# Cosine attention followed by a gated two-layer block on one core: new order tables for all engines

## The chip, the core and the metric

The kernel runs on one core of one Trainium2 chip. A core has a matrix engine (PE, with its weight loads shown apart as PEld), a vector engine (DVE), a scalar engine that evaluates functions (ACT), a slower general engine (POOL), and a queue engine (SP) that here issues only transfers. Every engine works through its own instruction list in order, and lists meet only at semaphores. The metric is the device time of one execution in microseconds, the median of several runs.

## The reference

```python
q, k, v: (8, 12, 448, 64) float32, tau = 0.1
q_n = q / (norm(q) + 1e-6);  k_n = k / (norm(k) + 1e-6)
attn = softmax(q_n @ k_n^T / tau)            # per batch and head, 448 x 448
x = (attn @ v) laid out as (8*448, 12*64)    # 3584 tokens x 768
h = x @ w_in                                 # 768 -> 2048
out = (h * cos(h)) @ w_out                   # 2048 -> 768, float32
```

## The kernel before

**Units of work.** A quad is a group of four heads of one batch, so there are 24 quads (numbers 0 to 23), three to a batch. For each quad q and k are loaded (`load_one`, L447, SP's queue) and v too (`load_v`, L461, POOL's queue); they are squared (`square`, L487), summed (L509), turned into inverse norms by a few tiny instructions (`inverse`, L516: ACT L527 and L539, DVE L542 and L545), scaled (`scale`, L547) and turned by a transfer (`turn`, L595). Then come seven steps of `scores` (L608), each four matmuls on PE (L619) and one exponential on ACT (L627), and seven steps of `attend` (L639, PE L646), whose result ACT or DVE copies out of PSUM (L656 or L659). The row sums of quads 0 to 5 are formed by `spread` (L663, PE L672) and inverted on ACT (L685, L689); those of later quads by rounds of two quads (`sums`, L726, PE L735), after DVE has added some of the exponential tiles up (`add_up`, L704, L722). POOL or DVE multiplies the sums' inverse in (L762), which gives x.

**Chunks.** A chunk is one batch of 448 tokens, numbers 0 to 7. Its first matmul (M1, L784) makes 16 blocks of 128 features in pairs. Each pair goes through ACT L797, DVE L799, ACT L801 and DVE L803, which leave h*cos(h) in `gT`. Its second matmul (M2, L815) makes 6 or 8 output blocks of 128 tokens by 384, 16 matmuls each; each finished block is copied to `osb` by ACT (L824) or DVE (L827) and stored. M2 blocks use PSUM banks 6 and 7; scores, spread and attend steps take the other three pairs of banks in turn (`next_pair`, L882), so that a step needs the bank pair of the third step before it to have been read out.

**Weaving.** While M2 of chunk c runs, PE also does the scores and attends of quads that a later chunk needs. `stream` is the list of slots: s is one scores step, v all seven attend steps of the quad before, z its spread. For chunk c the table `VISITS[c]` has pairs (n, m): do the next n slots, then m matmuls of M2 (L1163 to L1171). `LATER` moves the v and z of a quad within the slots of the next quad (L878). A round of sums is put in where L1139 and L1168 allow it. PE's order after the start is thus written down by these tables. The order on the other engines after the start comes from a planner (`pass_`, L144), which walks the operations with assumed durations and picks for each engine the operation that can start first, with a priority that follows from when PE needs it. `ENG` says on which engine an operation lies: keys `s0:q` and `s1:q` are the squares of q and k of quad q (POOL without an entry), `n0`/`n1` their scaling (POOL, and DVE for n1 of quads 4 to 7), `a` the copy of the attend result (DVE), `x` the last multiplication (POOL, DVE for quad 8), `o:t:h` the copy of output block h of tile t (DVE). `TREE` says how many exponential tiles of a quad DVE adds up ahead of its round: 0 leaves seven tiles to sum on PE, 4 leaves three, 5 two, 6 one.

**The start.** Until M1 of chunk 0 (quads 0 to 2 are done there whole), every engine's order is written out by hand (L936 to L1087). Operations are numbered in the order in which they are written, `MOVE` adds a number to some of them (L91), and each engine's list is sorted by the result (L137, L157). All POOL transfers keep such a place too. Weights come in four transfers of w_in (`load_w1`, L469) and four of w_out (`load_w2`, L477) on POOL's queue. The loads of quad 5 wait for the second transfer of w_out (L1037), those of quad 6 for the third and fourth (L1091).

```python
        if key is None:
            self.count += 1
            key = self.count - 1
            if self.strict:
                key += MOVE.get(key, 0)
...
        for n, more in plan[1:]:
            visit(stream[:n])
            del stream[:n]
            if due and at[0] >= 2 * NNB and 1 <= at[0] % NNB <= 12:
                round_(due.pop(0), 13 - cur[0])
            fill(more)
```

## Time and profile before

| quantity | value |
|---|---|
| median of 3 runs | 417.64 us (416.97 to 417.76) |
| the profiled execution's own time | 417.37 us |
| its span, first to last instruction | 415.6 us |
| PE busy | 406.9 us |
| ACT busy | 313.7 us |
| DVE busy | 306.6 us |
| POOL busy | 199.6 us |
| granted PE clock | 1.00 |

A share of busy time is a mean over stages. The table of stretches gives it for a chosen stretch; the list by time gives single instructions, merged where the same line repeats; the number in brackets behind a row is the engine's idle time ahead of it, and what ended that. PE rows overlap a little, because matmuls are pipelined.

### The profile page before, as it was taken

How to read it: one execution, taken by the hardware profiler on the slowest of the kernel's cores; microseconds unless marked ns; L12 is line 12 of the kernel's file. 1: busy time of each engine (PE TensorE's matmuls, PEld its weight loads, DVE VectorE, ACT ScalarE, POOL GpSimd, SP SyncE). 2: the span in 40 equal slices, each digit the busy share in tenths (PEclk: the TensorE clock that was granted, in tenths of full speed). 3: DMA queues.
4: the chain of work that ended last, by engine and by line, in shares of the span. 5: the costliest groups of instructions: out<-in, count | busy, mean ns of one | idle time of the engine just before them, and what ended most of it. 6: DMA issues, size and time to landing. Idle time of an engine off the chain costs nothing.

```text
span 415.6 us, 8581 instructions
## 1 busy us (share of the span) xinstructions
PE 406.9 (98%) x3600; PEld 217.5 (52%) x3601; DVE 306.6 (74%) x368; ACT 313.7 (75%) x417; POOL 199.6 (48%) x132
## 2 busy tenths in 40 slices
PE   7999999999999999999999999999999999999996
PEld 6674544445554455454555555454555555555563
DVE  4958997879853669963899899964988479836931
ACT  5998889988888987878878667889886667715700
POOL 3866329793386862688715495088504050030000
PEclk9999999999999999999999999999999999999999
DMA  8999999986099999199939689299803350071033
GB/s 267 231 244 209 236 225 275 217 180 152 4 205 168 262 236 237 40 177 244 188 113 176 132 181 219 33 162 211 178 2 82 77 108 22 1 165 39 0 77 76
DMA packets 71399, 62.83 MB, mean 151 GB/s; under 512 B 40512, under 2 KB 66240, under 8 KB 71360
## 3 DMA queue, kind: packets, MB, share of 16 engines
q1 hardware_dynamic: 60688, 50.09, 52.3%
q0 software_dynamic: 10240, 11.80, 17.6%
q8 instruction: 28, 0.46, 0.5%
q10 hardware_dynamic: 432, 0.39, 0.3%
q14 instruction: 11, 0.09, 0.1%
HBM read 45.61 MB, written 11.01 MB: 136 GB/s over the span
## 4 chain that ended last, share of the span: by engine, by line
PE 88%; ACT 8%; DVE 1%; DMA 1%; issue 0%; SPq 0%; DVEq 0%
PE PS L815 35%; PE PS L784 35%; PE PS L619 8%; PE PS L646 6%; ACT E L627 5%; PE PS L735 2%; PE PS L672 1%; DMA Kf<-in_k_dram 1%; ACT E L634 1%; ACT ar L689 1%; ACT ar L685 1%; PE PS L582 0%; DVE n L509 0%; DVE AVs L659 0%; DVE Qn L553 0%
## 5 line engine op out<-in xcount | busy, mean ns | idle before, releaser
L815 PE MATMUL PS<-W,gT 128*128 128x384 bf16 (+2 forms) x895 | 156.4, 327 | 0.1
L627 ACT ACTIVATE E<-PS 128x896 f16<-128x896 f32 x161 | 137.0, 917 | 21.8 <-PE PS L619 21.2
L784 PE MATMUL PS<-xT,W 128*128 128x448 bf16 x768 | 147.0, 352 | 0.0
L815 PEld LDWEIGHTS PS<-W,gT 128*128 128x128 bf16 x896 | 83.2, 98 | 69.1 <-issue 15.2
L784 PEld LDWEIGHTS PS<-xT,W 128*128 128x128 bf16 x768 | 74.7, 98 | 70.0 <-issue 0.4
L797 ACT ACTIVATE ar<-PS 128x896 int32<-128x896 f32 x64 | 58.2, 911 | 32.1 <-PE PS L784 31.4
L799 DVE SCALAR_TENSOR_TENSOR ar<-ar,PS 128x896 f32<-128x896 int32 x64 | 69.0, 1084 | 17.9 <-ACT ar L797 17.7
L803 DVE TENSOR_TENSOR gT<-PS,ar 128x896 bf16<-128x896 f32 x64 | 69.3, 1088 | 4.9 <-ACT ar L801 4.3
L801 ACT ACTIVATE ar<-ar 128x896 f32<-128x896 f32 x64 | 60.5, 947 | 16.0 <-DVE ar L799 15.3
L762 POOL TENSOR_TENSOR xT<-AVs,R 128x896 bf16<-128x896 f32 x17 | 37.9, 2231 | 57.4 <-DMA R<-Zs 57.4
L827 DVE COPY osb<-PS 128x384 f32<-128x384 f32 (+2 forms) x56 | 31.1, 554 | 41.6 <-PE PS L815 40.7
L505 POOL TENSOR_TENSOR sqq<-Qf 128x896 bf16<-128x896 f32 x21 | 35.3, 1680 | 44.4 <-DVE n L509 35.1
L619 PE MATMUL PS<-qT,kT 64*64 64x448 bf16 x672 | 51.0, 360 | 2.1 <-ACT E L627 1.2
L553 POOL TENSOR_TENSOR Qn<-Qf,rr 128x896 bf16<-128x896 f32 x20 | 37.9, 1897 | 29.7 <-DVE rr L545 25.7
L722 DVE TENSOR_TENSOR E<-E 128x1792 f16<-128x1792 f16 (+2 forms) x26 | 36.5, 1403 | 4.7 <-PE PS L646 4.5
L646 PE MATMUL PS<-E,Vb 64*64 64x448 f16 x672 | 37.7, 350 | 0.0
L505 POOL TENSOR_TENSOR sqk<-Kf 128x896 bf16<-128x896 f32 x17 | 30.5, 1797 | 13.6 <-DVE n L509 10.7
L553 POOL TENSOR_TENSOR Kn<-Kf,rr 128x896 bf16<-128x896 f32 x17 | 31.2, 1835 | 6.0 <-DVE Qn L553 3.6
L659 DVE COPY AVs<-PS 128x896 f32<-128x896 f32 x21 | 22.8, 1087 | 11.7 <-PE PS L646 11.5
L619 PEld LDWEIGHTS PS<-qT,kT 64*64 64x64 bf16 x672 | 16.3, 105 | 28.0 <-issue 11.3
L509 DVE TENSOR_REDUCE n<-sqq 128x14 f32<-128x896 bf16 (+2 forms) x23 | 23.7, 1035 | 6.8 <-POOL sqq L505 6.0
L646 PEld LDWEIGHTS PS<-E,Vb 64*64 64x64 bf16 x672 | 20.0, 107 | 11.8 <-ACT E L627 0.9
(57 smaller groups left out, 232.8 us busy)
## 6 DMA issues: line engine op xcount, KB each, us to landing
out_dram<-osb SPq DMA_DIRECT2D x54, 192.0 KB, 3.0
Qf<-in_q_dram SPq DMA_DIRECT2D x23, 448.0 KB, 5.1
Kf<-in_k_dram SPq DMA_DIRECT2D x23, 448.0 KB, 5.1
R<-Zs SPq DMA_DIRECT2D x72, 112.0 KB, 3.0
Vb<-in_v_dram POOLq DMA_DIRECT2D x24, 224.0 KB, 5.2
W<-in_moe_w_in_dram POOLq DMA_DIRECT2D x4, 768.0 KB, 17.3
W<-in_moe_w_out_dram POOLq DMA_DIRECT2D x4, 768.0 KB, 25.1
qT<-Qn SPq DMA_TRANSPOSE x20, 4.3
```

What stands on the lines that cost most here:

```text
L505: op(eng, (1.68 if eng == "pool" else 1.05) * n, lambda e: e.tensor_tensor(dst, src, src, ALU.mult), r=cut(nm + "f", s, part), w=own, afte ...
L553: lambda e: e.tensor_tensor(n[0].ap()[:, j0:j1].rearrange("p j r d -> p r j d"), f[s].ap()[:, :, j0:j1], rb, ALU.mult),
L619: ins = e.matmul(bank(bs + r, S, 64 * a, 64 * a + 64), kT[u].ap()[64 * r:64 * r + 64, j, a, :], qT[u].ap()[64 * r:64 * r + 64, :, a, :], s ...
L627: act("exp", 0.81, lambda e: e.activation(E.ap()[:, es], two(bs), ACT.Exp, bias=SHIFT, scale=INV_TAU), r=pair(bs), w=[("E", es)], chain="E")
L646: ins = e.matmul(bank(bk + a, S, 64 * r, 64 * r + 64), Vb[vs].ap()[64 * a:64 * a + 64, r, j, :], E.ap()[64 * a:64 * a + 64, es, r, :], sta ...
L762: op(eng, 2.04 if eng == "pool" else 1.05, lambda e, u=u, sl=sl, b=b, c0=c0: e.tensor_tensor(xT[b % 2].ap()[:, c0:c0 + 2, :], AVs[sl].ap() ...
L784: ins = e.matmul(bank(bk + i2), W1.ap()[:, i, 128 * nb:128 * nb + 128], xT[c % 2].ap()[:, i, :], start=(i == 0), stop=(i == NKC - 1))
L797: op("act", 0.815, lambda e: e.activation(ar[s].ap().bitcast(I32), two(bk), ACT.Identity, bias=0.25, scale=INV2PI), r=bs, w=[("ar", s)], a ...
L799: op("dve", 1.005, lambda e: e.scalar_tensor_tensor(ar[s].ap(), ar[s].ap().bitcast(I32), -2.0 * math.pi, two(bk), ALU.mult, ALU.add), r=bs ...
L801: act("sin", 0.86, lambda e: e.activation(ar[s].ap(), ar[s].ap(), ACT.Sin, bias=GUARD * math.pi / 2.0, scale=GUARD), r=[("ar", s)], w=[("a ...
L803: op("dve", 1.01, lambda e: e.tensor_tensor(gT.ap()[:, 2 * pr:2 * pr + 2, col:col + S], two(bk), ar[s].ap(), ALU.mult), r=bs + [("ar", s)] ...
L815: ins = e.matmul(bank(bk, x1 - x0), gT.ap()[:, f, col:col + 128], W2.ap()[:, f, x0:x1], start=(f == 0), stop=(f == NNB - 1))
```

## The change

Five tables get new values; no instruction is written anew and no wait is written by hand.

- `VISITS` and `LATER`: other cuts of the same slots. Written out with s, v and z, chunk 1 for example ends before with ... [s s v10 s] 4 [s s] 6 [s s] and M1, and after with ... [s] 7 [s s] 9 [s s v10 s s s s s] 4 and M1. Chunk 0 begins with 23 instead of 25 matmuls of M2. Chunk 4 has [s v19 s s], a round, [s s] where it had [s s v19 s s], a round, [s s s] (the rounds are put in by L1168). A run of slots between two runs of M2 counts as one trip; there are 51 trips in both tables (11, 11, 6, 8, 7, 8 before; 10, 12, 6, 8, 7, 8 after, by chunk).
- `ENG`: 19 of the 56 output copies and 6 of the 21 attend copies go from DVE to ACT. Eight scalings, five last multiplications and four squares go from POOL to DVE. Of the four squares on ACT three go to POOL and one to DVE; one other goes from POOL to ACT.
- `TREE`: quad 22 gets 6 for 5, quad 12 gets 4 for 3.
- `MOVE`: every operation of the start gets a number. On SP, k of quads 3, 4 and 5 is loaded before q. On ACT, in the chain of inverse norms of quad 0, the last step for q (L536) goes ahead of the first for k, and the two last tiny steps for the second half of k (L534 and L536) go ahead of the first exponential, where they were behind the second and third. The two tiny steps of quad 3 (L527, L539) go ahead of the inversion of quad 2's sums (L685, L689), where they were behind it. On PE, the last spread of quad 2 goes behind its last attend. On POOL, the loads of v of quads 1 and 2 go behind two of the weights. The transfers of weights go out in the order w_in 2, 3, w_in 1, w_out 2, w_in 4, w_out 3, w_out 1, and w_out 4 only after three squares of quads 3 and 4; v of quad 3 goes out ahead of w_out 3 instead of behind all weights.

```diff
 VISITS = [
-    [(0, 25), (3, 12), (3, 11), (3, 3), (3, 5), (3, 12), (3, 10), (3, 4), (3, 4), (3, 0), (3, 4), (3, 5), (1, 1)],
-    [(0, 20), (3, 11), (3, 13), (3, 13), (3, 0), (3, 15), (3, 11), (3, 8), (6, 0), (3, 16), (2, 11), (4, 4), (2, 6),
-        (2, 0)],
-    [(0, 26), (2, 11), (3, 0), (2, 20), (4, 11), (3, 9), (2, 10), (5, 0), (3, 2)],
-    [(0, 21), (3, 9), (3, 11), (3, 8), (2, 8), (4, 26), (4, 17), (2, 12), (3, 11)],
-    [(0, 19), (3, 7), (3, 7), (2, 15), (3, 9), (3, 12), (2, 17), (5, 0), (2, 0), (1, 12)],
-    [(0, 25), (4, 15), (3, 21), (3, 15), (5, 24), (3, 7), (1, 10), (4, 8), (2, 14)],
+    [(0, 23), (3, 15), (3, 6), (2, 5), (5, 4), (2, 12), (3, 7), (2, 8), (5, 8), (6, 5), (3, 0)],
+    [(0, 23), (3, 5), (2, 16), (3, 8), (2, 4), (3, 0), (3, 14), (2, 10), (3, 11), (5, 12), (3, 6), (1, 7), (2, 9), (8,
+        4)],
+    [(0, 22), (3, 11), (2, 0), (3, 18), (3, 3), (2, 14), (3, 19), (5, 0), (3, 2)],
+    [(0, 19), (3, 10), (3, 12), (2, 0), (1, 8), (2, 7), (4, 28), (4, 20), (3, 12), (2, 7)],
+    [(0, 19), (3, 13), (3, 18), (3, 16), (4, 11), (3, 10), (2, 5), (4, 0), (2, 15)],
+    [(0, 25), (4, 6), (3, 14), (3, 17), (4, 26), (3, 23), (3, 9), (2, 10), (3, 10)],
     [],
     [],
 ]
...
-LATER = {18: -1, 5: 3, 7: -1, 21: -1, 9: 4, 10: -2, 12: 0, 23: 2, 15: -2, 13: -1, 22: 2, 8: 1, 16: 2, 14: 0, 17: -1,
-    19: -1, 20: 0}
+LATER = {18: -2, 5: 3, 7: -2, 21: 0, 9: 4, 10: -2, 12: -1, 23: 5, 15: -2, 13: 0, 22: 2, 8: 0, 16: 2, 14: 0, 17: -1,
+    19: 1, 20: 1, 3: -1, 4: 0, 11: 0}
...
-MOVE = {49: 2.0, 100: -6.5, 94: -4.0, 199: 5.5, 198: 3.0, 48: -155.0, 123: 23.0, 33: -18.5, 21: -15.0, 149: -9.5, 143:
...
+    18: 3.664, 19: 6.11, 20: 8.62, 21: 4.938, 22: 7.615, 23: 9.894, 24: 16.08, 25: 22.556, 26: 2.596, 27: 6.258, 28:
+    6.866, 29: 7.474, 30: 8.082, 31: 13.382, 32: 13.99, 33: -14.07, 34: 13.598, 35: 14.206, 36: 2.802, 37: 5.33, 38:
+    1.63, 39: -16.508, 40: 6.77, 41: 8.584, 42: 1.17, 43: 2.93, 44: -10.022, 45: 4.926, 46: 5.534, 47: 6.142, 48:
...
+    96: -9.342, 97: -6.424, 98: -2.99, 99: 3.888, 100: -14.752, 101: -5.45, 102: -15.69, 103: 2.63, 104: -26.57, 105:
+    -14.19, 106: 76.208, 107: -9.122, 108: -7.662, 109: -9.364, 110: -6.842, 111: -13.962, 112: -5.89, 113: -6.236,
...
-ENG = {'s1:13': 'act', 's1:21': 'act', 's1:22': 'act', 's1:23': 'act', 'o:3:1': 'dve', 'n1:12': 'dve', 'o:5:1': 'dve',
-    's0:15': 'pool', 's1:14': 'pool', 's0:20': 'pool', 'o:14:0': 'dve', 'o:16:1': 'dve', 'n0:20': 'pool', 'n1:19':
-    'pool'}
-TREE = {12: 3, 11: 0, 13: 0, 16: 4, 14: 6, 15: 6, 17: 4, 18: 2, 19: 0, 23: 6, 20: 6, 22: 5, 21: 6}
+ENG = {'s1:13': 'pool', 's1:21': 'dve', 's1:22': 'pool', 's1:23': 'pool', 'o:3:1': 'act', 'n1:12': 'dve', 'o:5:1':
+    'act', 's0:15': 'pool', 's1:14': 'dve', 's0:20': 'pool', 'o:14:0': 'dve', 'o:16:1': 'act', 'n0:20': 'pool',
+    'n1:19': 'pool', 'o:2:0': 'act', 'a:8': 'dve', 'n1:8': 'pool', 's0:9': 'pool', 'o:3:0': 'dve', 'o:6:0': 'act',
...
+    's1:10': 'pool', 'x:7': 'pool', 'n1:10': 'pool', 'a:7': 'dve', 's0:11': 'pool', 'n1:9': 'dve', 'n1:16': 'pool',
+    'x:12': 'pool'}
+TREE = {12: 4, 11: 0, 13: 0, 16: 4, 14: 6, 15: 6, 17: 4, 18: 2, 19: 0, 23: 6, 20: 6, 22: 6, 21: 6, 10: 0, 8: 0, 9: 0}
```

2 lines of the change are left out of this document (added), and 40 rows, old and new, of tables (ENG, MOVE).

## The prediction

> **What bounds the kernel now.** I read the page's busy times and the shares of the chain that ended last, then that chain in order of time, then the table of stretches. The page:
>
> ```profile
> PE 406.9 (98%) x3600; PEld 217.5 (52%) x3601; DVE 306.6 (74%) x368; ACT 313.7 (75%) x417; POOL 199.6 (48%) x132
> PE 88%; ACT 8%; DVE 1%; DMA 1%; issue 0%; SPq 0%; DVEq 0%
> ```
>
> PE carries 88% of the chain and ACT 8%. The chain in order of time gives what PE's work costs where nothing holds it up:
>
> ```profile
> 113.23 2.22 PE PS L815 x13
> 115.45 0.69 PE PS L619 x12
> 118.86 1.32 PE PS L646 x28
> 120.19 1.44 PE PS L735 x28
> ...
> 182.32 4.16 ACT E L627 x5
> ...
> 192.67 18.16 PE PS L784 x96
> 391.50 15.60 PE PS L815 x96
> ```
>
> M1 of a chunk takes 18.16 us. An M2 matmul takes 15.60/96 = 0.1625 us, an attend step (four matmuls) 1.32/7 = 0.189, a step of a round 1.44/7 = 0.206, and an exponential on a busy ACT 4.16/5 = 0.83. I take 0.189 for a scores step too. A trip from M2 to three scores and back costs (2.22 - 13 x 0.1625) + (0.69 - 3 x 0.189) = 0.11 + 0.12 = 0.23 us beyond its matmuls. The table of stretches (length, then busy time of PE, PEld, DVE, ACT, POOL) shows where PE is not the bound:
>
> ```profile
> 11.10:34.60 23.50, 21.70 (x397) 15.00 (x393) 17.72 (x27) 23.27 (x38) 17.61 (x18) 1.00 1.11 235
> 58.70:88.80 30.10, 29.67 (x360) 14.09 (x349) 24.52 (x32) 29.72 (x42) 23.47 (x13) 1.00 0.95 220
> 105.57:145.85 40.28, 40.07 (x465) 19.94 (x464) 24.96 (x35) 36.22 (x53) 27.74 (x19) 1.00 0.83 167
> ```
>
> Between 11.1 and 34.6 ACT works 23.27 of 23.50 us (PE's busy time there holds filler matmuls), and between 58.7 and 88.8, the scores of chunk 0, 29.72 of 30.10. In the weaving of chunk 1 ACT has 4 us to spare and DVE 15. So the limits are ACT in the start and in chunk 0, and PE afterwards; later PE stalls are a few tenths each.
>
> **The change part by part.** PE's matmuls are the same except for one step of a round: `TREE` leaves quad 22 one tile instead of two, which shortens the last round by one step, **-0.2 us**. The trips number 51 in both tables, so 51 x 0.23 us neither comes nor goes; the gain can only be stalls.
>
> *The start.* ACT's and PE's rows by time (start, length, row; in brackets the idle time ahead):
>
> ```profile
> 7.53 0.21 ACT L534 ACTIVATE nrm<-nrm 128x14 f32<-128x14 f32 x1
> ...
> 8.25 0.20 ACT L536 ACTIVATE rr<-nrm 128x14 f32<-128x14 f32 x1
> ...
> 10.68 0.57 PE L619 MATMUL PS<-qT,kT 64*64 64x448 bf16 x8
> 11.12 2.21 ACT L634 ACTIVATE E<-PS,rr 128x448 f16<-128x448 f32 x4 [1.25 <-PE PS L619]
> 13.61 0.19 ACT L534 ACTIVATE nrm<-nrm 128x6 f32<-128x6 f32 x1
> 13.71 1.14 ACT L634 ACTIVATE E<-PS,rr 128x448 f16<-128x448 f32 x2
> 14.74 0.20 ACT L536 ACTIVATE rr<-nrm 128x6 f32<-128x6 f32 x1
> 14.84 4.57 ACT L634 ACTIVATE E<-PS,rr 128x448 f16<-128x448 f32 x8
> ...
> 35.04 0.92 ACT L685 ACTIVATE ar<-PS 128x896 f32<-128x896 f32 x1 [0.49 <-PE PS L672]
> 35.11 5.85 PE L784 MATMUL PS<-xT,W 128*128 128x448 bf16 x30
> 37.71 1.28 ACT L424 ACT_TABLE_LOAD   x1
> ```
>
> The step that yields q's inverse norm starts at 8.25, though the one before it in q's chain (7.53) ends at 7.74: two steps for k stand between. Put ahead of them it can gain at most 0.51 us; I take half, since another tiny step is put into the chain. q's scaling, turning and the first scores (10.68) hang on it, so the first exponential (11.12) comes 0.25 earlier, out of 1.25 us that ACT idles there. The steps at 13.61 and 14.74 each push the next exponential back by 0.1 us (13.71 - 13.61, 14.84 - 14.74); moved into that idle time they free 0.2. The spread that goes behind an attend on PE holds L685 up by one attend step, 0.19, but quad 3's tiny steps then fit into the 0.49 us that ACT idles before 35.04, so the table load comes earlier still. Sum 0.25 + 0.2 + 0.2 - 0.19, **-0.45 us**. The bounds are -0.85 (no loss by the spread, and twice the 0.2 at the table load) and +0.2 (nothing gained, the spread's price stays).
>
> *The weights.* They set no time before, and their new order is the risk of the start. For one transfer each: its issue, and the time to its landing, of the third weight (13.3) and the fourth (14.0), and of the last (21.4, the longest of the fourth row):
>
> ```profile
> L474 POOL DMA_DIRECT2D W<-in_moe_w_in_dram x1: 696/696/696, 13.3 to 13.3; - x1
> DMA to landing us min/median/max: 19.7/19.7/19.7
> ...
> L474 POOL DMA_DIRECT2D W<-in_moe_w_in_dram x4: 669/692/726, 11.2 to 14.0; - x4
> DMA to landing us min/median/max: 9.9/17.3/22.7
> ...
> L479 POOL DMA_DIRECT2D W<-in_moe_w_out_dram x4: 762/768/819, 19.1 to 21.4; - x4
> DMA to landing us min/median/max: 20.7/25.1/32.0
> ```
>
> They land at 33.0, 36.7 and 53.4. M1 needs w_in 1 and 2 from its start, which was 35.11 and becomes 34.6. In the new order w_in 1 is the third weight out, with the same v loads and weights ahead as the third before, so I take 33.0: 1.6 us to spare, cost 0, and 36.7 - 34.6 = 2.1 if it fares like the fourth. w_out 4 is issued some ten microseconds later, behind three squares, but stands behind seven weights as before, plus one v; I take 55, and it is needed only after the first visit of chunk 0, after 58. w_out 2, for which SP holds the loads of quad 5 and all behind them, goes out fourth instead of sixth, so those loads come earlier; w_out 4 holds those of quad 6 a little longer. PE waits for none of them, **0**.
>
> *Chunk 0.* The list by time, where chunk 0 begins and ends, and from the groups the nearest row to an output copy on ACT:
>
> ```profile
> 58.79 2.54 ACT L627 ACTIVATE E<-PS 128x896 f16<-128x896 f32 x3 [0.20 <-PE PS L619]
> ...
> 87.08 1.73 ACT L627 ACTIVATE E<-PS 128x896 f16<-128x896 f32 x2
> 87.25 0.92 PE L784 MATMUL PS<-xT,W 128*128 128x448 bf16 x4
> ...
> L750 ACT ACTIVATE Zs<-PS 128x448 f32<-128x448 f32 x9 | 4.9, 543 | 2.0 <-PE PS L735 1.9
> L827 DVE COPY osb<-PS 128x384 f32<-128x384 f32 (+2 forms) x56 | 31.1, 554 | 41.6 <-PE PS L815 40.7
> ```
>
> M1 of chunk 1 starts with two exponentials left, so ACT's end sets it. The first visit two M2 matmuls earlier saves at most the 0.20 us. Two of chunk 0's copies that come to ACT are ready well before its end; the copy has no row on ACT, its price lies between 0 (put behind the exponentials) and 0.543, the row of 448 instead of 384 columns; I take 0.5, the row it is nearest to, for one and 0 for the other. **+0.35 us** (0.5 - 0.15), bounds -0.2 and +0.9. DVE loses the copies' 0.554 each and was not the bound there.
>
> *Chunk 1.* Its end becomes one run of eight slots with quad 10's attend in third place; before it was cut in three:
>
> ```profile
> 143.89 0.38 PE L619 MATMUL PS<-qT,kT 64*64 64x448 bf16 x4 [0.21 <-DVE AVs L659]
> ```
>
> With three bank pairs the seventh scores step needs the fourth exponential done: 4 x 0.83 + 0.35 (first scores to exponential) = 3.7 us, while PE's own work ahead of it is 6 x 0.189 + 1.32 = 2.45. That is a stall of 1.2, less two trips (0.46) and the old wait (0.21), though chunk 1 has one trip more elsewhere (0.23): 0.76. ACT may begin the run with less or no queue before M2's last matmuls and M1 takes part of it, so I take half, **+0.4 us**, bounds -0.4 and +1.2. ACT gets five output copies here, 5 x 0.543 = 2.7 of its 4 spare us: covered; if not, they are a rival. Eight operations come to DVE, and five copies leave it; what they cost is worked out with the lock below.
>
> *Chunks 2 to 5.* PE stalls that have a row:
>
> ```profile
> 169.32 1.21 DVE L827 COPY osb<-PS 128x384 f32<-128x384 f32 x2
> 169.93 0.60 PEld L815 LDWEIGHTS PS<-W,gT 128*128 128x128 bf16 x5 [0.39 <-DVE osb L827]
> 283.19 0.87 PE L619 MATMUL PS<-qT,kT 64*64 64x448 bf16 x8
> ```
>
> At 169.93 PE waits for two copies in a row on DVE; of tile 7 one is now on ACT, -0.35. At 283.19 two scores steps take 0.87 instead of 0.57, because a bank pair is still being read; chunk 4's new cut avoids it, -0.3. Together **-0.65 us**, bounds -1.3 (the like in chunks 3 and 5 too) and +1.5 (new stalls of that size at one trip in eight, 0.35 x 4). Six attend copies go to ACT and quad 12's and 22's added sums to DVE, beside PE's work; if that cover goes, the rounds and x come later, more than a chunk ahead of their use.
>
> Sum: -0.2 - 0.45 + 0 + 0.35 + 0.4 - 0.65 = **-0.55 us**. The profiled execution took 417.37, 0.27 under the median of 417.64; I put the forecast between 417.37 - 0.55 = 416.8 and 417.64 - 0.55 = 417.1, at **416.9**.
>
> **The lock between DVE and POOL.** Rows of the scalings:
>
> ```profile
> L553 POOL TENSOR_TENSOR Qn<-Qf,rr x20: 1679/1688/2593, 41.5 to 314.3; 128x896 bf16<-128x896 f32 x20
> ...
> L553 DVE TENSOR_TENSOR Kn<-Kf,rr x4: 1081/1092/1673, 62.5 to 143.8; 128x896 bf16<-128x896 f32 x4
> ```
>
> A scaling on POOL takes 1.69 us, at worst 2.59; on DVE 1.09, at worst 1.67. So now and then one engine waits for the other, by 0.6 to 0.9 us. In chunk 1 DVE gets 8 x 1.09 and loses 5 x 0.554, +5.9 of its 15 spare us. At 0.6 of waiting each, chunk 1's eight moved operations cost DVE 4.8 us more, which still fits: 24.96 + 5.9 + 4.8 = 35.7 of 40.28. [...]
>
> **The rivals.**
> 1. The stalls add up to a clear gain: the start at its bound (-0.85), copies behind the exponentials (-0.2), the run of eight hidden (-0.4), -0.65 and -0.2: -2.3, 415.2. For it: ACT idles 1.25 us at 11.12. Against: every term at its good end.
> 2. Slower by late weights: w_in 1 lands after 34.6 and PE waits in front of M1. At 36.7 that is 2.1 us: 416.9 + 2.1 = 419.0. It decides from a landing at 35.3, 0.7 us late, which undoes the forecast's gain against the median. For it: weights land 3.7 us apart (33.0 to 36.7), so one place back is enough. Against: 1.6 us to spare.
> [...]
> 4. Slower by ACT's queue: its 2.7 us of output copies in chunk 1 fall behind exponentials, M2's banks come free late, and half of it, with the run's full 1.2 instead of 0.4, reaches PE: 416.9 + 1.35 + 0.8 = 419.
> 5. The new order does nothing that counts: 417.5; this lies within the forecast's own spread.
>
> **How the numbers follow.** What a measurement of this kernel can tell from no change is 0.2%, 0.8 us, thus 416.8 and 418.5. The forecast with its own range (415.9 to 418.2, rival 5 in it) has 0.42, of which 0.17 falls below 416.8; rival 1 has 0.25, rival 2 0.13, rival 3 0.07, rival 4 0.13. Faster 0.17 + 0.25 = 0.42, same 0.25, slower 0.33. The range from 414.6 to 420.5 leaves out rival 3 and the far ends of 1 and 2.
>
> **What would show it.** In the profile after: the first L634 before 11.0, with no tiny step between it and the next ones; M1's first L784 near 34.6 with no wait for a weight; chunk 0's scores with ACT still full; two scores steps of 0.6 in chunk 4's end; a wait for L627 of about a microsecond at the end of chunk 1. Wrong would make it: a transfer that ends an idle time of PE, PE idle for more than a microsecond in one place of chunks 1 to 5, or M1 slower than 18.2 in any chunk.

## The result and the profile after

The changed kernel took 422.31 us, the median of 10 runs (418.66 to 427.61), against 417.56 (416.71 to 420.1) for the kernel before, run beside it. The ratio is 1.0102, with a 95% interval of 1.0067 to 1.0137: slower by about 1%, where 416.9 was forecast and 420.5 was the upper end of the range. One run of the ten, 427.61, counts as slow and is left out of the ratio. The time also spreads far more than before, and it goes roughly with the granted PE clock of the run: 418.66 at a clock of 1.000, 420.14 and 420.89 at 0.999, 421.63 to 422.67 at 0.995 and 0.996, 422.37 to 424.85 at 0.991 and 0.992.

The profiled execution took 422.67 us, with a span of 420.6. All line numbers of the changed kernel are 26 higher (M1 is L810, M2 L841, scores L645, their exponential L653, attend L672, its copy on DVE L685, scaling L579, square L531). The page of the changed kernel, busy times and shares of the chain that ended last:

```profile
PE 408.4 (97%) x3597; PEld 216.3 (51%) x3597; DVE 313.1 (74%) x363; ACT 323.0 (77%) x439; POOL 173.4 (41%) x117
PE 74%; ACT 12%; DMA 4%; DVE 3%; POOL 3%; issue 3%; SPq 0%; POOLq 0%; DVEq 0%
```

PE's busy time rose by 1.5 us, although its rounds of sums have four matmuls fewer (152 for 156), and PE's share of the chain fell from 88% to 74%; a transfer, DVE and POOL stand in it now. Where the time went is read from the start of M1's first row in each chunk in the list by time; the differences are the lengths of the stages:

| kernel | median (runs) | M1 of chunk 0 starts | chunk 0 | chunk 1 | chunk 4 | chunk 5 | chunk 6 |
|---|---|---|---|---|---|---|---|
| before | 417.56 (10) | 35.11 | 52.14 | 58.54 | 46.14 | 50.99 | 34.35 |
| after | 422.31 (10) | 35.48 | 52.29 | 64.43 | 45.67 | 50.36 | 34.18 |

Chunk 1 costs 5.9 us more, the start 0.4 and chunk 0 0.15; chunks 4 to 6 give back 0.47 + 0.63 + 0.17, chunks 2 and 3 are equal to 0.1. The table of stretches for chunk 1 (length, then busy time of PE, PEld, DVE, ACT, POOL, then the granted clock), first of the kernel before:

```profile
87.30:145.80 58.50, 58.29 (x562) 29.33 (x561) 41.05 (x53) 50.53 (x69) 36.96 (x25) 1.00 0.77 167
```

and of the changed kernel:

```profile
87.80:152.20 64.40, 60.38 (x561) 29.56 (x561) 45.57 (x54) 52.40 (x75) 32.11 (x20) 0.97 0.83 160
```

No engine is full: DVE is busy for 45.57 of 64.40 us. PE is idle for 4.0 us (64.40 - 60.38) where it was for 0.2, and its work takes 2.1 us longer, at a mean clock of 0.97. The chain of the changed kernel there, in order of time (start, length, what):

```profile
122.19 10.26 DMA qT<-Qn
...
132.54 1.09 DVE Qn L579
133.63 1.00 DVE Kn L579
...
135.63 1.01 DVE AVs L685
...
136.68 0.50 PE PS L645 x4
```

and the same place in its list by time:

```profile
131.96 1.57 PE L672 MATMUL PS<-E,Vb 64*64 64x448 f16 x28
132.54 1.09 DVE L579 TENSOR_TENSOR Qn<-Qf,rr 128x896 bf16<-128x896 f32 x1 [2.96 <-DMA qT<-Qn]
...
135.55 2.08 DVE L685 COPY AVs<-PS 128x896 f32<-128x896 f32 x2
136.68 0.50 PE L645 MATMUL PS<-qT,kT 64*64 64x448 bf16 x4 [3.14 <-DVE AVs L685]
```

The scaling of quad 11's q (`n0:11`) was moved from POOL to DVE. There is one tile `Qn` for all quads, so this scaling may not write before the turn transfer of quad 10's q has read it, and that transfer landed only at 132.5, 10.26 us after its issue. In the kernel before the same scaling waited for the same transfer on POOL, which cost nothing (list by time of the kernel before):

```profile
125.85 1.69 POOL L553 TENSOR_TENSOR Qn<-Qf,rr 128x896 bf16<-128x896 f32 x1 [0.75 <-DMA qT<-Qn]
```

In the changed kernel DVE stands for 2.96 us, and behind it in DVE's list stand k's scaling, a sum, and the attend copies of quads 8 and 9. PE needs the bank pair of quad 8's attend for its next scores and idles 3.14 us. Then its clock drops; the table of stretches of the changed kernel, for PE alone:

```profile
136.00:137.00 1.00, 0.32 (x4) 0.91 0.17 38
137.00:138.00 1.00, 1.00 (x16) 0.50 1.11 216
138.00:139.00 1.00, 1.00 (x20) 0.50 0.87 110
139.00:140.00 1.00, 1.00 (x13) 0.50 0.69 192
140.00:141.00 1.00, 1.00 (x6) 0.89 1.05 403
```

The averages amount to some 3.4 us at a clock of 0.50, about 1.7 us of lost work by these numbers; the 28 matmuls of the round there take 2.81 us (L761 at 137.11), where those of the round at 120.91, at a clock of 1.00, take 1.51. The start lost in a like manner, on a smaller scale. The list by time of the changed kernel:

```profile
10.47 0.63 ACT L660 ACTIVATE E<-PS,rr 128x448 f16<-128x448 f32 x1
15.17 2.17 DVE L579 TENSOR_TENSOR Kn<-Kf,rr 128x512 bf16<-128x512 f32 x1
...
17.40 0.40 PE L608 MATMUL PS<-ident,Kn 128*128 128x128 bf16 x4 [0.70 <-DVE Kn L579]
...
19.26 0.38 PE L645 MATMUL PS<-qT,kT 64*64 64x448 bf16 x4 [0.97 <-DVE kT L618]
```

The first exponential came at 10.47, 0.65 us earlier than before. But the scaling of the first half of quad 1's k, which PE needs first, now stands behind the second half and behind q (a move that the list of the change above leaves out), and takes 2.17 us on DVE, where it took 0.69 before; k's turned tile is late, and the gain is gone. The list by time of the kernel before:

```profile
14.34 0.69 DVE L553 TENSOR_TENSOR Kn<-Kf,rr 128x512 bf16<-128x512 f32 x1
```

### The profile page after: what moved, and what is told of

The parts are those of the page before. It is cut to its first block, busy times and chain, and to the rows that moved or that the text cites. A ratio compares the mean times of both kernels' runs of the same rounds, so it can differ in the third digit from the quotient of the medians.

```text
span 420.6 us, 8576 instructions
## 1 busy us (share of the span) xinstructions
PE 408.4 (97%) x3597; PEld 216.3 (51%) x3597; DVE 313.1 (74%) x363; ACT 323.0 (77%) x439; POOL 173.4 (41%) x117
## 4 chain that ended last, share of the span: by engine, by line
PE 74%; ACT 12%; DMA 4%; DVE 3%; POOL 3%; issue 3%; SPq 0%; POOLq 0%; DVEq 0%
PE PS L810 32%; PE PS L841 29%; ACT E L653 9%; PE PS L645 6%; PE PS L672 4%; DMA qT<-Qn 2%; PE PS L761 2%; DMA Kf<-in_k_dram 2%; ACT ar L715 1%; ACT ar L711 1%; POOL Qn L579 1%; POOL sqk L531 1%; DVE Qn L579 1%; DVE Kn L579 1%; DVE n L535 1%
## 5 line engine op out<-in xcount | busy, mean ns | idle before, releaser
L841 PE MATMUL PS<-W,gT 128*128 128x384 bf16 (+2 forms) x896 | 156.5, 327 | 0.0
L653 ACT ACTIVATE E<-PS 128x896 f16<-128x896 f32 x161 | 137.0, 920 | 17.6 <-PE PS L645 16.8
L810 PE MATMUL PS<-xT,W 128*128 128x448 bf16 x768 | 147.2, 353 | 0.0
L841 PEld LDWEIGHTS PS<-W,gT 128*128 128x128 bf16 x896 | 83.3, 98 | 69.4 <-issue 16.6
L810 PEld LDWEIGHTS PS<-xT,W 128*128 128x128 bf16 x768 | 74.5, 98 | 70.5 <-issue 0.7
L823 ACT ACTIVATE ar<-PS 128x896 int32<-128x896 f32 x64 | 58.2, 911 | 32.5 <-PE PS L810 31.9
L788 POOL TENSOR_TENSOR xT<-AVs,R 128x896 bf16<-128x896 f32 x12 | 25.8, 2146 | 85.9 <-DMA R<-Zs 85.9
L645 PE MATMUL PS<-qT,kT 64*64 64x448 bf16 x672 | 49.9, 360 | 6.1 <-DVE AVs L685 3.6
L853 DVE COPY osb<-PS 128x384 f32<-128x384 f32 (+2 forms) x37 | 20.5, 553 | 36.5 <-PE PS L841 36.0
L531 POOL TENSOR_TENSOR sqk<-Kf 128x896 bf16<-128x896 f32 x18 | 31.8, 1769 | 27.0 <-DVE n L535 20.5
L579 POOL TENSOR_TENSOR Qn<-Qf,rr 128x896 bf16<-128x896 f32 x17 | 35.8, 2107 | 16.8 <-DVE rr L571 11.0
L531 POOL TENSOR_TENSOR sqq<-Qf 128x896 bf16<-128x896 f32 x18 | 31.4, 1742 | 27.3 <-DVE n L535 14.4
L672 PE MATMUL PS<-E,Vb 64*64 64x448 f16 x672 | 37.4, 350 | 0.0
L748 DVE TENSOR_TENSOR E<-E 128x1792 f16<-128x1792 f16 (+2 forms) x28 | 34.5, 1243 | 3.7 <-PE PS L672 3.5
L490 POOL DMA_DIRECT2D Vb<-in_v_dram x24 | 18.0, 753 | 37.2 <-PE PS L645 35.5
L645 PEld LDWEIGHTS PS<-qT,kT 64*64 64x64 bf16 x672 | 16.1, 105 | 31.8 <-issue 9.8
L672 PEld LDWEIGHTS PS<-E,Vb 64*64 64x64 bf16 x672 | 19.3, 107 | 13.4 <-issue 1.2
L535 DVE TENSOR_REDUCE n<-sqk 128x14 f32<-128x896 bf16 (+2 forms) x23 | 23.8, 1033 | 1.0 <-POOL sqk L531 0.8
```

The source lines that it names most:

```text
L531: op(eng, (1.68 if eng == "pool" else 1.05) * n, lambda e: e.tensor_tensor(dst, src, src, ALU.mult), r=cut(nm + "f", s, part), w=own, afte ...
L535: return op("dve", 0.07 + 0.95 * n, lambda e: e.tensor_reduce(out=n2.ap()[:, u, H * w:H * w + H] if part == ALL[0] else jr(n2, u, w, part) ...
L579: lambda e: e.tensor_tensor(n[0].ap()[:, j0:j1].rearrange("p j r d -> p r j d"), f[s].ap()[:, :, j0:j1], rb, ALU.mult),
L645: ins = e.matmul(bank(bs + r, S, 64 * a, 64 * a + 64), kT[u].ap()[64 * r:64 * r + 64, j, a, :], qT[u].ap()[64 * r:64 * r + 64, :, a, :], s ...
L653: act("exp", 0.81, lambda e: e.activation(E.ap()[:, es], two(bs), ACT.Exp, bias=SHIFT, scale=INV_TAU), r=pair(bs), w=[("E", es)], chain="E")
L672: ins = e.matmul(bank(bk + a, S, 64 * r, 64 * r + 64), Vb[vs].ap()[64 * a:64 * a + 64, r, j, :], E.ap()[64 * a:64 * a + 64, es, r, :], sta ...
```

## The experiments

Unless the text says otherwise, a kernel below is the changed kernel (or the one before) with the order of every engine frozen as planned and single operations moved in it, so that nothing else shifts. The function that does it stands ahead of the emission of the instructions:

```diff
+    def settle(self):
+        ops, done, line = self.ops, set(), {e: [o for o in self.order if o.eng == e] for e in self.ENGINES}
+        for i, eng, at in SWAPS:
+            line[ops[i].eng].remove(ops[i]); ops[i].eng = eng; line[eng].insert(line[eng].index(ops[at]), ops[i])
...
```

An entry (operation, engine, other) moves an operation to that engine, ahead of the other; waits are derived anew from the tiles read and written. The stages of all kernels, read as above; a single profile of each, the medians of all its runs:

| kernel | median (runs) | M1 of chunk 0 starts | chunk 0 | chunk 1 |
|---|---|---|---|---|
| a1_copies_first | 426.05 (5) | 35.33 | 52.29 | 66.01 |
| a2_q11_pool | 420.21 (12) | 39.30 | 52.29 | 60.91 |
| a3_v11_later | 420.45 (12) | 35.86 | 52.29 | 60.20 |
| a4_fill | 422.45 (5) | 38.85 | 52.29 | 62.54 |
| d1_before_q11 | 416.98 (12) | 34.62 | 52.13 | 58.20 |
| d2_before_q11_late | 419.15 (5) | 35.02 | 52.14 | 60.38 |
| b1_halves | 419.64 (6) | 34.30 | 52.30 | 61.12 |
| b2_square_later | 421.13 (6) | 35.49 | 52.29 | 63.83 |
| d3_before_halves | 418.38 (12) | 35.57 | 52.14 | 58.75 |
| f1_second_first_q | 419.02 (1) | 35.19 | 52.30 | 60.95 |
| f2_q_first_second | 416.56 (1) | 33.97 | 52.30 | 59.80 |
| f3_square_earlier | 421.33 (1) | 38.85 | 52.29 | 59.51 |
| b3_three | 416.56 (12) | 34.11 | 52.30 | 59.50 |
| b4_hybrid | 416.16 (12) | 34.64 | 52.14 | 59.01 |
| c1_best | 415.91 (5) | 33.85 | 52.31 | 59.62 |

The kernel before stood at 417.31, 417.24 and 417.31 beside the a, b and c/d runs (22 or 23 runs each), and at 416.86 (one run) beside f. The three f kernels ran once, so their times decide nothing; only their profiles are used. Kernels with the same chunk 1 as before (b4, d3, and d1 in all but two operations) show 58.2 to 59.0 for it, so less than 0.8 us of chunk 1's length is no difference. The unchanged start of before, d1, d2 and b4 lies between 34.62 and 35.11.

**Chunk 1: the order on DVE (a1_copies_first).** Operations 667 and 678 are the copies of quads 8 and 9, 635 and 636 the scalings of quad 11.

```diff
+SWAPS = [(667, 'dve', 635), (678, 'dve', 636)]
```

> The changed kernel with every engine's order kept, except that on DVE the attend copies of quads 8 and 9 stand ahead of the scaling of quad 11's q and of its k. Theory (DVE stands in order at that scaling until quad 10's turn transfer has read Qn, and the copies that PE needs stand behind it): PE's idle 3.14 us in chunk 1 goes, the low granted clock of the next 4 us (about 1.7 us) goes with it, so 422.3 - 4.8 = 417.5, chunk 1 (M1's first matmul to the next one's) 64.4 -> 59.6. Rival, the new cuts of chunk 1 or ACT's output copies cost the 5.9 us: 422 still, chunk 1 64. Rival, two engines that block each other (DVE and POOL): 422, since as many of DVE's operations meet POOL's.

It took 426.05, ratio 1.0203 (1.0165 to 1.024): the expectation failed. The copies are in time, and the wait has moved on. The list by time of a1_copies_first:

```profile
134.85 1.98 DVE L579 TENSOR_TENSOR Kn<-Kf,rr 128x896 bf16<-128x896 f32 x1
136.76 1.07 DVE L535 TENSOR_REDUCE n<-sqq 128x14 f32<-128x896 bf16 x1
137.86 0.23 ACT L553 ACTIVATE nrm<-n 128x28 f32<-128x28 f32 x1 [4.91 <-DVE n L535]
139.05 0.54 ACT L776 ACTIVATE Zs<-PS 128x448 f32<-128x448 f32 x1
139.64 2.42 PE L841 MATMUL PS<-W,gT 128*128 128x384 bf16 x7 [3.71 <-ACT Zs L776]
```

ACT now stands at a tiny step of quad 12's norm, which needs the sum that DVE does last; behind it waits the logarithm of the round, which alone frees the M2 bank that PE wants. What was cured for one engine's list was passed to the next one's.

**Chunk 1: the engine (a2_q11_pool) and the transfer (a3_v11_later).** Operation 614 is POOL's first multiplication there, 602 the load of quad 11's v, 684 the scaling of quad 12's q.

```diff
+SWAPS = [(635, 'pool', 614)]
```

> The changed kernel with every engine's order kept, except that the scaling of quad 11's q is on POOL, ahead of POOL's two multiplies that wait for R there. Theory (the wait for the turn transfer is harmless on POOL, which sits idle 10.26 us there, and harmful on DVE): 417.5 again, chunk 1 59.6, and POOL shows the wait. Rival, chunk 1's new cuts: 422. Rival, blocking between DVE and POOL: 422 or more, as POOL gets one more operation.

Chunk 1 fell from 64.43 to 60.91, where 59.6 was expected; at its end PE idles 1.36 us for another copy in this profile. The whole came to 420.21, ratio 1.0057 (1.0029 to 1.0085), not to 417.5. The profiled run, at a clock of 0.992, has a late start (below). Five of the six runs at a clock of 1.00 took 417.9 to 418.8, the four at 0.996 419.8 to 421.4, the two at 0.991 and 0.992 423. The list by time of a2_q11_pool, in chunk 1:

```profile
135.49 1.68 POOL L579 TENSOR_TENSOR Qn<-Qf,rr 128x896 bf16<-128x896 f32 x1 [7.54 <-DMA qT<-Qn]
135.81 1.09 DVE L685 COPY AVs<-PS 128x896 f32<-128x896 f32 x1 [1.08 <-PE PS L672]
```

POOL waits 7.54 us for the same transfer at no cost to PE, and DVE's copy follows its attend at once.

```diff
+SWAPS = [(602, 'pool', 684)]
```

> The changed kernel with every engine's order kept, except that POOL issues the load of quad 11's v after its two multiplies (near 139) and not at 123.38. What it asks is why the turn transfer of quad 10's q took 10.26 us. If the v load, issued 1.2 us after it, shares its time: it lands near 127 to 129, DVE's wait and PE's idle 3.14 us go, 417.5. If the loads, the store and the R transfers of SP's own queue delay it: landing stays near 132 and the time near 422. I hold the second a little likelier (0.55), as the loads and stores ahead of it in SP's queue carry 448 + 448 + 192 KB against 224 KB.

It took 420.45, ratio 1.007 (1.0047 to 1.0092), and 60.20 in chunk 1; the whole is again not the 417.5 of that branch. The transfer issues of a3_v11_later (microseconds to landing last) and its list by time:

```profile
qT<-Qn SPq DMA_TRANSPOSE x1, 7.1
```

```profile
130.27 1.09 DVE L579 TENSOR_TENSOR Qn<-Qf,rr 128x896 bf16<-128x896 f32 x1
...
134.41 0.38 PE L645 MATMUL PS<-qT,kT 64*64 64x448 bf16 x4 [0.49 <-DVE AVs L685]
```

7.1 us instead of 10.26 are enough: DVE no longer waits, and PE's 3.14 us are 0.49. That the load of v is what made the difference is not shown by this, though. The changed kernel and five of the kernels below keep its order in chunk 1, load of v included, and differ only in the start; the same transfer landed differently in each, and the waits follow it:

| kernel | transfer, issue to landing | DVE waits for it | PE idles for quad 8's copy | chunk 1 |
|---|---|---|---|---|
| after | 10.3 | 2.96 | 3.14 | 64.43 |
| b2_square_later | 9.8 | 3.10 | 2.50 | 63.83 |
| b1_halves | 8.8 | 2.02 | 1.42 | 61.12 |
| f1_second_first_q | 8.5 | 1.85 | 1.25 | 60.95 |
| f2_q_first_second | 7.3 | 0.70 | no wait listed | 59.80 |
| f3_square_earlier | 7.1 | 0.31 | no wait listed | 59.51 |

So the loss in chunk 1 goes with the late landing, and it is not in every execution. With the load of v in place the landing took 7.1 to 10.3 us in nine profiles (these six, a1, a2 and a4), with the load later 7.1 and 6.5 (a3, b3): the load may lengthen it, which is the side that I held less likely, but one profile with it was as short as a3's. In the kernel before the transfer took 4.1, and 5.8 in d1's profile; what the difference comes from (k's turn goes first now, and loads and a store stand ahead in SP's queue) was not taken apart.

**Chunk 1: what the clock costs (a4_fill).**

```diff
+            x == 70 and op("pe", 0.0, lambda e: products(e, 50, 6), r=["ident"], w=whole(6), mode="q"); scores(x, next_pair())
```

> The changed kernel with 50 small products (128x128, into a bank that is free there) on PE ahead of the scores of quad 10 that wait 3.14 us; nothing else moves. It leaves the wait and takes only PE's idle time. If the low granted clock from 136.1 to 140.1 follows from PE's idle time: the clock stays at 1.00 there and the time falls by about 1.7 us, 422.3 -> 420.6. If it has another cause: 422.3 or, if the products end after the copies, up to 0.5 more.

The time, 422.45, did not fall to the 420.6 expected. It decides little: the five runs have clocks of 0.991 to 0.996, so the clock fell somewhere in each, and in the profile it fell in the start (M1 at 38.85). In that profile chunk 1 took 62.54. The products held PE up for 2.97 us (the transfer landed after 8.4 us here, so the idle time that they replace was shorter than 3.14), and the table of stretches of a4_fill shows the clock still at 1.00 where they end:

```profile
139.00:140.00 1.00, 1.00 (x19) 1.00 1.22 193
```

So a hold-up of nearly the same length costs 1.9 us less where PE is kept busy. The other way to about the same number: chunk 1 without the wait took 59.50 (b3_three below), plus 3.14 is 62.64, and the changed kernel took 64.43, 1.8 more.

**The same place in the kernel before (d1_before_q11, d2_before_q11_late).** In the kernel before, operations 635 and 636 are the scalings of quad 11, 668 the copy of quad 8, 579 the turn of quad 10's q, 613 the fifth transfer of R.

```diff
+SWAPS = [(635, 'dve', 668), (636, 'dve', 668)]
```

> The kernel before, with every engine's order kept, except that the scalings of quad 11's q and k stand on DVE ahead of the attend copies of quads 8 and 9, as in the changed kernel. In the kernel before the turn transfer of quad 10's q had landed by 125.85, so DVE would run them at about 125.9 to 128 and be idle again when the first attend product ends at 131.4. Theory (the place costs only with a late transfer): 417.2, chunk 1 58.5. Rival, DVE's added work costs by itself, or meets POOL's: 418 or more, with copies that start later than 131.4.

416.98, ratio 0.9996 (0.9986 to 1.0007): no difference. The list by time of d1_before_q11:

```profile
127.10 1.08 DVE L553 TENSOR_TENSOR Qn<-Qf,rr 128x896 bf16<-128x896 f32 x1
...
130.87 1.09 DVE L659 COPY AVs<-PS 128x896 f32<-128x896 f32 x1 [1.68 <-PE PS L646]
```

```diff
+SWAPS = [(635, 'dve', 668), (636, 'dve', 668), (579, 'sp', 613)]
```

> As the kernel before this one, and SP issues the turn of quad 10's q behind the first four transfers of R, near 127 instead of 121.7, so that it lands near 131.3. Theory: DVE waits there, the two scalings end near 133.4, the copy of quad 8 ends near 134.5 and PE, which wants its bank at 132.7, idles 1.8 us; chunk 1 60.3, the whole 419 (and up to 1.7 more where the clock falls). If the wait on DVE does not hold PE up: 417.2. If PE instead waits for the late qT itself: the row of the scores names the DMA.

419.15, ratio 1.0039 (1.0026 to 1.0053), with chunk 1 at 60.38: as expected. The list by time of d2_before_q11_late:

```profile
129.71 2.09 POOL L762 TENSOR_TENSOR xT<-AVs,R 128x896 bf16<-128x896 f32 x1 [4.22 <-DMA R<-Zs]
130.62 2.13 DVE L553 TENSOR_TENSOR Qn<-Qf,rr 128x896 bf16<-128x896 f32 x1 [3.02 <-DMA qT<-Qn]
...
134.81 0.57 PE L619 MATMUL PS<-qT,kT 64*64 64x448 bf16 x8 [1.99 <-DVE AVs L659]
```

It takes both: the scaling on DVE ahead of the copies, and a late transfer. The place alone is free (d1), and so is a late transfer, 9.5 us, with the scaling on POOL (a2). PE's 1.99 us here were not followed by a fall of the clock (1.00 in the table of stretches from 134 to 138).

**The start: order of the halves (b1_halves, d3_before_halves).** Operations 83 and 97 are the first and second half of quad 1's k scaling, 82 that of q, 103 the square of quad 2's q on DVE, 104 that of its k on POOL, which waits for 97.

```diff
+SWAPS = [(83, 'dve', 97), (97, 'dve', 103)]
```

> The changed kernel with every engine's order kept, except that on DVE the two halves of quad 1's k scaling change places (first half first, as in the kernel before); the square of quad 2's k on POOL waits for the second half, as it did. Theory (DVE and POOL shut each other out where both have two inputs from SBUF: the square of q on DVE and that of k on POOL start within 0.4 us of each other, and where POOL is first DVE's takes 2.56 us instead of 1.08, the copy of kT is late, PE idles 2.45 us and its clock falls): POOL's square now comes after DVE's has begun, so the event is gone in every run, M1's first matmul comes near 34.9 (35.5 without, 39.0 with the event), no run of the ten shows the 3.4 us, and the median falls from 422.3 to about 420.5, what is left being chunk 1. Rival, DVE's scaling of 2.17 us against 0.69 is the cause by itself: it stays 2.17 wherever the half stands if it belongs to the operation, and the first M1 stays at 35.5 or 39. Rival, the start plays no part: 422.

419.64, ratio 1.0071 (1.0047 to 1.0095). The first M1 comes at 34.30, and the first half takes 0.69 us again:

```profile
13.88 0.69 DVE L579 TENSOR_TENSOR Kn<-Kf,rr 128x512 bf16<-128x512 f32 x1
14.49 1.08 DVE L579 TENSOR_TENSOR Qn<-Qf,rr 128x896 bf16<-128x896 f32 x1
15.49 0.55 DVE L579 TENSOR_TENSOR Kn<-Kf,rr 128x384 bf16<-128x384 f32 x1
```

(the list by time of b1_halves). So the 2.17 us do not belong to that half. The start alone is worth 1.2 us against the changed kernel's profile, and it is 0.3 to 0.8 better than in the four profiles with the start of before.

```diff
+SWAPS = [(97, 'dve', 83), (83, 'dve', 103)]
```

> The kernel before, with every engine's order kept, except that the halves of quad 1's k scaling stand on DVE in the changed kernel's order (second half, q, first half). POOL's square of quad 2's k, which waits for the second half, is let go near 14.9 instead of 16.5 and then runs beside DVE's scalings. Theory (shutting out): one of DVE's scalings or POOL's square takes 1 to 1.7 us longer, quad 1's k is late by as much, PE idles about 1 us near 17 and the first M1 comes at 36 to 36.5, in the bad case with the clock's fall at 39; 418.3 to 421. If the first half in third place takes 2.17 us by itself: the same size, but without an overlap with POOL. If neither: 417.2.

418.38, ratio 1.0026 (1.0015 to 1.0038): this order alone makes the kernel before slower by 1.1 us, with M1 at 35.57 where 36 to 36.5 was expected, and its first half, in third place, takes 2.17 us there too. The list by time of d3_before_halves:

```profile
14.51 2.36 POOL L505 TENSOR_TENSOR E<-Kf 128x896 bf16<-128x896 f32 x1
15.25 2.17 DVE L553 TENSOR_TENSOR Kn<-Kf,rr 128x512 bf16<-128x512 f32 x1
```

Here POOL's square of k, let go early by the second half, runs beside the scaling, which ends 0.55 us after it (16.87 to 17.42): the two shut each other out. In the changed kernel the scaling is just as long (15.17 to 17.34), but the record has no such operation of POOL beside it, only issues of transfers; POOL's square starts at 17.34.

**The start: which square comes first (b2_square_later, f3_square_earlier).** In two of the profiles above, a2 and a4, M1 began 3.4 to 3.8 us later than in the changed kernel's. The list by time of a2_q11_pool, in the start, and its table of stretches for PE:

```profile
16.90 2.00 POOL L531 TENSOR_TENSOR E<-Kf 128x896 bf16<-128x896 f32 x1
17.29 2.56 DVE L531 TENSOR_TENSOR E<-Qf 128x896 bf16<-128x896 f32 x1
...
20.77 0.59 PE L645 MATMUL PS<-qT,kT 64*64 64x448 bf16 x4 [2.45 <-DVE kT L618]
```

```profile
20.00:22.00 2.00, 1.23 (x11) 0.50 1.06 192
22.00:24.00 2.00, 2.00 (x28) 0.50 1.14 277
```

POOL's square of k starts 0.4 us ahead of DVE's square of q, and DVE's ends 0.95 us after POOL's (18.90 to 19.85), 1.5 us late; a4 shows the same (POOL first by 0.38 us, DVE's 2.56). In the changed kernel's own profile DVE was first by 0.08 us, and POOL's square took 2.54 instead of the 1.75 of b1. Operations 106 and 108 are loads of w_out on POOL.

```diff
+SWAPS = [(106, 'pool', 104)]
```

> The changed kernel with every engine's order kept, except that POOL issues the last load of w_out ahead of the square of quad 2's k and not behind it, so that the square starts near 18.0 instead of 16.9 to 17.3. Theory (whichever of DVE's and POOL's squares starts first shuts the other out): DVE's, at 17.1 to 17.3, is always first, its time stays 1.08, the start stays at 35.5 in every run, and the spread shrinks as in the kernel with the halves changed; the median falls to about 421. If the order of the two squares does not matter: M1's first matmul at 39 in about half the runs, and 422.3.

421.13, ratio 1.0101 (1.008 to 1.0123), the start at 35.49, as expected; but the six runs' remaining spread (420.2 to 423.5) is that of chunk 1, where PE idled 2.50 us in the profile, and they can't show by themselves that the late start never came.

```diff
+SWAPS = [(104, 'pool', 108)]
```

> The changed kernel, with POOL's square of quad 2's k ahead of the last but one load of w_out, so that it runs from about 16.5 to 18.2 and DVE's square of q, due at 17.3, always comes second. Theory (whoever starts second waits for the end of the other): DVE's square takes 1.9 to 2.0 us (18.2 + 1.08 - 17.3), the copy of kT is 0.9 later, PE idles 1.8 us in front of the scores of quad 1 instead of 0.97, first M1 36.4; with the clock's fall, if 1.8 us of idle time are enough for it, 38. If the two do not shut each other out: DVE's square 1.08, first M1 35.5.

The late start came, at 38.85, with the clock's fall, but not by the step that I expected. The list by time of f3_square_earlier:

```profile
15.12 3.24 DVE L579 TENSOR_TENSOR Kn<-Kf,rr 128x512 bf16<-128x512 f32 x1
16.05 1.75 POOL L531 TENSOR_TENSOR E<-Kf 128x896 bf16<-128x896 f32 x1
...
18.28 1.08 DVE L531 TENSOR_TENSOR E<-Qf 128x896 bf16<-128x896 f32 x1
18.42 0.40 PE L608 MATMUL PS<-ident,Kn 128*128 128x128 bf16 x4 [1.78 <-DVE Kn L579]
...
20.28 0.59 PE L645 MATMUL PS<-qT,kT 64*64 64x448 bf16 x4 [0.96 <-DVE kT L618]
```

POOL's square got in ahead of the slow scaling, which ended 0.56 us after it (17.80 to 18.36); DVE's square found POOL's done.

**The start: why 2.17 us (f1_second_first_q, f2_q_first_second).**

```diff
+SWAPS = [(83, 'dve', 82)]
```

> The changed kernel, with DVE's three scalings of quad 1 in the order second half of k, first half of k, q (second half, q, first half in the changed kernel). The first half took 0.69 us where it stood first and 2.17 where it stood third. If it is slow because the second half ran before it: 2.17 again, from 14.2 on. If because it stands third, behind q: 0.69, and q's scaling takes its place at 1.08 or is slow itself. The time of one execution, 419 to 423, decides nothing.

```diff
+SWAPS = [(82, 'dve', 97), (83, 'dve', 97)]
```

> The changed kernel, with DVE's three scalings of quad 1 in the order q, first half of k, second half. If the first half is slow where the second ran before it: 0.69 here. If it is slow where q ran before it: 2.17 here. If what is slow is whatever runs near 15.2 us (a time, not an order): the second half, at about 15.3, takes 1.5 us more than its 0.55.

In f1 the two halves ran in 1.16 us together and it was q, now third, that took 2.57 instead of 1.08; in f2, as in b1, all three were at their usual length. So it is neither the operation nor the moment: in these runs the scaling that stood third took 1.5 us longer where the second half of k was first (after, d3, f1), and none did where that half was last (b1, f2). In d3 POOL's square explains it. In the changed kernel and f1 POOL only issues transfers meanwhile, as it does in f2 and b1, where nothing is held; what holds DVE there stays open. The slow orders have in common that the second half, for which POOL's square waits, is done early; no run took that square away.

**Put together (b3_three, b4_hybrid, c1_best).** The changed kernel with the three places undone (halves, scaling of quad 11, load of v):

```diff
+SWAPS = [(83, 'dve', 97), (97, 'dve', 103), (635, 'pool', 614), (602, 'pool', 684)]
```

> The changed kernel with three places undone and all else kept: the halves of quad 1's k scaling in the old order, the scaling of quad 11's q on POOL, the load of quad 11's v behind POOL's two multiplies. Theory (the loss is these places, not the new cuts as such): start 34.9, chunk 0 52.3, chunk 1 60.2 to 60.9, chunks 4 to 6 1.3 us shorter than before: 417.3 - 0.2 + 0.2 + 1.9 - 1.3 = 417.9, with a narrow spread. Rival, the new cuts cost by themselves: 420 or more.

416.56, 12 runs, eleven of them between 416.26 and 417.25, where 417.9 was expected; ratio 0.9995 (0.9982 to 1.0008), the same as before, and 5.75 us under the changed kernel. The three places together carry the whole loss; the new tables as a whole cost nothing, since what chunks 0 and 1 still lose (0.16 and 1.0 us in the profiles) the start and chunks 4 to 6 give back.

The kernel before with the changed `VISITS`, `LATER`, `ENG` and `TREE` for chunks 4 and 5, planned anew:

```diff
-    [(0, 19), (3, 7), (3, 7), (2, 15), (3, 9), (3, 12), (2, 17), (5, 0), (2, 0), (1, 12)],
-    [(0, 25), (4, 15), (3, 21), (3, 15), (5, 24), (3, 7), (1, 10), (4, 8), (2, 14)],
+    [(0, 19), (3, 13), (3, 18), (3, 16), (4, 11), (3, 10), (2, 5), (4, 0), (2, 15)],
+    [(0, 25), (4, 6), (3, 14), (3, 17), (4, 26), (3, 23), (3, 9), (2, 10), (3, 10)],
...
```

> The kernel before, with the changed tables for chunks 4 and 5 alone (visits, places, engines and sums of quads 16 to 23). The two traces showed chunk 4 shorter by 0.46, chunk 5 by 0.63 and chunk 6 by 0.17. If these are gains of these tables: 417.3 - 1.25 = 416.05. If they came only from the other state in which the earlier chunks of the changed kernel left the engines: 417.3, or slower.

416.16, ratio 0.9975 (0.9949 to 1.0001): the size expected (416.05), with an interval that just touches no change. Chunks 4, 5 and 6 took 45.67, 50.36 and 34.18, as in the changed kernel.

The same with the changed `MOVE` and the halves in their old order:

```diff
+SWAPS = [(83, 'dve', 97), (97, 'dve', 103)]
```

> The kernel before with two parts of the change: the changed start, in it the two halves of quad 1's k scaling in the order of before, and the changed tables for chunks 4 and 5. Chunks 0 to 3 are those of before. If the gains are separate and add up: the first M1 at 34.1 to 34.3 instead of 35.1 (as with the halves mended in the changed kernel), chunks 4 to 6 shorter by 1.25, 417.2 - 0.9 - 1.25 = 415.1. If the earlier start only moves a wait into chunk 0: 416.1, as the tables for chunks 4 and 5 gave alone.

415.91, ratio 0.9961 (0.9947 to 0.9975), five runs within 0.6 us: faster than both kernels by 0.4% and 1.5%. The first M1 stands at 33.85, but chunk 1 took 59.62 here, so part of the earlier start was not kept, and 415.1 was missed by 0.8.

## Why the prediction was wrong

**Chunk 1, the step that failed.** The move of operations to DVE was put at nothing, because their busy time fits. The prediction says: "Eight operations come to DVE, and five copies leave it; what they cost is worked out with the lock below", and there: "+5.9 of its 15 spare us". The load was sized well enough (DVE's busy time rose by 4.5 us and had room), but load was the wrong measure. An operation that is moved takes its waits along, and these then hold up everything behind it in the new engine's list, here DVE's for 2.96 us and through it PE for 3.14. The one `Qn` tile, the transfer that reads it, and the two attend copies behind the scaling were all in the code and in the list by time; POOL's wait for that transfer, 0.75 us, stood in the profile of before and cost nothing there. The case was among those named as "Wrong would make it", PE idle for more than a microsecond in one place of chunks 1 to 5, but it had no rival and no price. In the profile the price was 3.1 us of idle time and about 1.8 of clock, 4.9 of the 5.9 us that chunk 1 lost, and a spread, since the landing varies from 7.1 to 10.3 us. That the wait is the cause is shown from both sides: it goes with the landing in six kernels, it goes when the scaling is back on POOL (a2, b3), and the kernel before gets it when place and late landing are both put in (d2) and not by the place alone (d1). The +0.4 us for the run of eight slots was of the right size but only in part of the right kind: with the wait gone a wait of 0.25 for an exponential is left there, which it named, and one of 0.50 for a copy, which it did not. Chunk 1 takes 59.5, 0.5 to 1.3 more than in the four profiles with the chunk of before.

**The start.** The -0.45 us were reckoned on quad 0's chain alone, and that part came out better: the first exponential 0.65 earlier. What failed is the step that stopped there. The moved order of DVE's three scalings of quad 1 was not among the parts costed, and it took more than the gain: +0.37 in the profile, and 3.4 to 3.8 more in the two profiles in which POOL's square comes first. With the halves in their old order M1 starts at 34.30, 34.11 and 33.85 (b1, b3, c1) against 34.62 to 35.11 with the start of before, 0.8 better in the mean, where 0.45 was forecast. That the order of the scalings causes it is shown (b1, d3); what holds the third scaling in the changed kernel is not.

**What held.** No wait of PE names a weight (rival 2 out, weights 0). Chunk 0 cost +0.15, forecast +0.35. The last round gave the 0.17 of the -0.2. Chunks 2 to 5 gave 1.16 in sum against -0.65, in chunks 4 and 5, not in 2. The -0.35 for two copies in chunk 2 did not come: it took 46.72 in both. Without the three places the median is 416.56 against 417.24 beside it, -0.7, where -0.55 was forecast; the interval of the ratio includes no change, and the nearness of the two numbers is in part luck, since the start and chunks 4 and 5 gained more than forecast and chunk 1 lost more.

**The rivals.** The 0.07 of rival 3, at 421, stood for a wait of DVE for POOL of 1.69 us in each of the eight operations that come to it in chunk 1. No run shows such waits: in the changed kernel's chunk 1 seven of DVE's eight scalings, squares and multiplications took 1.08 to 1.13 us and one 2.64 (L531 at 142.54, beside POOL's square), and DVE was never the bound (45.57 of 64.40 us). Operations of DVE and POOL do shut each other out; where it showed a price was at one place in the start, 1.5 us for a square (a2, a4). Rival 4 (ACT's queue) fell: chunk 1 with all of ACT's copies takes 59.5. Rival 1's 415.2 was not reached even without the three places (416.56).

## What to carry to other kernels

When an operation moves to another engine, look up what it waits for and what then stands behind it in that list, before adding up busy times; here 7.54 us of such a wait on a transfer cost PE nothing on POOL, which was idle (a2), and 2.96 us of it cost PE 3.14 on DVE, which hands out PSUM banks. Price such a wait with PE's clock in it: here the clock fell after idle times of 2.45 us and more, and the work that followed at a clock of 0.50 added some 1.7 us to a wait of 3.14. And where two engines' list positions race within tenths of a microsecond, fix the order by a dependency, or the median hides two different executions, here with M1 at 35.5 us (after) and at 38.9 and 39.3 (a4, a2) behind the same start.
